# w_in loaded in f32 chunks and cast on chip, V of batch 0 summed per head pair, cast engines chosen anew

## The chip, the core and the metric

The kernel runs on one core of a Trainium2 chip. A core has TensorE (PE, matrix products, with weight loads shown apart as PEld), VectorE (DVE), ScalarE (ACT), GpSimd (POOL) and SyncE (SP), which here only issues DMAs. TensorE writes to PSUM; the other data lives in SBUF, 128 partitions wide. The metric is the device time of one execution in microseconds, lower is better. The kernel before took 215.6 us in the median of six runs (213.97 to 217.12).

## The reference

Attention with a causal window of 64 keys (8 batches, 8 heads, 576 positions, head size 64), followed by a gated unit that mixes positions with a spatial matrix. All inputs and the output are float32.

```python
def _attn_ref(q, k, v):
    scores = np.matmul(q, k.transpose(0, 1, 3, 2)) / np.sqrt(64)
    rel = pos[:, None] - pos[None, :]
    scores = np.where((rel >= 0) & (rel < 64), scores, -1e9)
    attn = np.exp(scores - np.max(scores, axis=-1, keepdims=True))
    attn = attn / (np.sum(attn, axis=-1, keepdims=True) + 1e-09)
    return np.matmul(attn, v)

def _moe_ref(x, w_in, w_spatial, b_spatial, w_out):   # x: (8, 576, 512)
    h = np.maximum(x @ w_in, 0.0)                     # w_in: 512 x 1024
    u, v = h[..., :512], h[..., 512:]
    v_n = (v - mean(v)) / np.sqrt(var(v) + 1e-06)     # over the last axis
    v_s = np.einsum('ts,bsd->btd', w_spatial, v_n) + b_spatial[None, :, None]
    return (u * v_s) @ w_out                          # w_out: 512 x 512
```

## The kernel before, in words

Nothing is scheduled automatically. One string, `ORDER` (line 20), lists some 1,150 steps; lines 644 to 646 read it word by word and call the function that each word names, with the numbers after the dots as arguments. Each engine runs its own instructions in exactly that order, so the string fixes all queues at once: a step that waits holds back everything behind it on its engine. A last letter P, D or A puts a copy on POOL, DVE or ACT.

The work of a batch `b`:

- **Loads** on SP: `l.b.x.s` (load, line 288; x is q or k) and `lv.b.n` (line 304). Batches 0 to 2 come in pieces of a head pair (s = 0 to 3, 256 KB, rows of 1 KB) and one piece with the last 64 positions of all heads (s = 4, 128 KB). From batch 3 on q and k come in eight pieces of one head (144 KB). V comes in pieces n, of one head (128 KB) or of 128 positions (256 KB). The f32 buffers (tags fq, fk, vf) exist twice, so batch b+2 waits for the casts of batch b.
- **Casts** to f16: `c.b.x.s.e` (line 317) for q and k, 512 elements wide per partition in batches 0 to 2 and 1152 wide after that; `cv.b.n.e` (line 330) for V; `sh.b.n.half.e` (line 339) copies V shifted by 64 rows.
- **Attention** of a head pair s (s = 4 is the last 64 positions of all): in batches 0 to 2 `T.b.x.s` transposes on TensorE and `to.b.x.s.e` copies the result out of PSUM; later `R.b.x.s` transposes on DVE. Then `S.b.s` scores on TensorE, `E.b.s` exp on ACT (tile e), `M.b.s` the mask as a minimum on DVE, `P.b.s` sums and values on TensorE (tile oz), `n1` and `n2` ln and exp on ACT (tiles ln, zi), `x.b.s` the product on DVE (tile x), which is pair s of the input to the gated unit.
- **Gated unit**: `V.b.j.r0.r1` (line 517) is 128 positions j times the right half of w_in; the sum over the 512 input columns runs in four parts r, part r being head pair r, and r0 to r1 says which of the parts are done by this word. `Q.b` does the last 64 positions of V and the last 64 of the output of the batch before. `vo` evicts V with a relu (tile vs), `bs` takes its mean and variance on DVE, `rs` and `ln` normalise it (tile vn). `U.b.m` (line 575) is the left half of w_in times x (tile pu), `ru` its relu on ACT. `G.b.m` is the spatial product (tile ps), `g` the gate on DVE, `O.b.j` the output product (tile po), `oc.b.j.e` (line 620) its copy into an f32 buffer (tag ob, five buffers), `st.b.j` (line 627) the store on SP.
- **Weights**: `win.half` (k_win, line 243) loads half of w_in with one gpsimd DMA that casts to f16 on the way. `wsp` and `wout` do so with the other two; `W.kk` and `wo.kk.e` turn the spatial matrix.
- **Warm-ups**: `H.n` runs n matmuls on a scratch tile.

Batch b's gated unit is interleaved with the attention of batch b+1 and the loads of later ones. In the order before, every `c`, `cv` and `sh` is on POOL but for five casts of batch 0, every `oc` on ACT, and every `vo` on ACT but for four. Eight SP DMAs can be in flight, each with a semaphore of its own: a ninth load waits for the landing of the one eight places before it.

The two halves of w_in were placed behind P of pair 0; V of batch 0 comes in the pieces 0 to 3 and 3 to 4:

```
... c.0.k.2.D lv.0.6 ... c.0.q.3.D win.1 H.3 to.0.q.1.A lv.0.8 n2.0.0 c.0.k.3.D win.0 ...
V.0.2.0.3 ... V.0.0.0.3 ... V.0.3.0.3 ... V.0.2.3.4 ... V.0.3.3.4 ... V.0.0.3.4 ... V.0.1.0.3 ... V.0.1.3.4
```

Of the kernel before, what the change touches and what calls it, by code (L numbers as in the profile page):

```python
# [14 lines left out]
S = 576  # L15
# [5 lines left out]
keep scratch l.0.k.1 H.4 id l.0.q.2 l.0.k.0 l.0.q.0 lv.0.0 H.6 l.0.k.2 lv.0.3 c.0.k.1.D lv.0.1 mask  # L21
c.0.q.2.P lv.0.2 H.3 maskr l.0.q.3 c.0.k.0.D c.0.q.0.P ones.0 l.0.q.4 T.0.k.0 l.0.k.3 to.0.k.0.D
T.0.q.0 l.0.q.1 H.2 to.0.q.0.A c.0.k.2.D lv.0.6 T.0.k.1 H.3 l.1.k.1 to.0.k.1.D S.0.0 l.1.q.0
cv.0.0.P E.0.0 sh.0.0.0.P lv.0.7 sh.0.0.1.P M.0.0 lv.0.5 cv.0.1.P small lv.0.4 P.0.0 sh.0.1.1.P
n1.0.0 T.0.k.2 c.0.q.1.P table T.0.q.2 lv.1.0 to.0.k.2.D sh.0.1.0.P T.0.q.1 l.0.k.4 c.0.q.3.D win.1
H.3 to.0.q.1.A lv.0.8 n2.0.0 c.0.k.3.D win.0 lv.1.2 to.0.q.2.A S.0.1 x.0.0 c.0.q.4.P l.1.q.1 H.2
E.0.1 T.0.q.3 cv.0.3.P lv.1.1 T.0.k.3 S.0.2 to.0.q.3.A l.1.k.0 M.0.1 cv.0.2.P E.0.2 to.0.k.3.D P.0.1
sh.0.2.0.P n1.0.1 H.2 M.0.2 sh.0.3.0.P S.0.3 n2.0.1 H.4 E.0.3 x.0.1 lv.1.3 c.0.k.4.P sh.0.2.1.P
P.0.2 M.0.3 n1.0.2 sh.0.3.1.P T.0.q.4 n2.0.2 T.0.k.4 P.0.3 to.0.q.4.A x.0.2 cv.0.4.P n1.0.3
V.0.2.0.3 to.0.k.4.D c.1.q.0.P n2.0.3 V.0.0.0.3 sh.0.4.0.P ones.1 x.0.3 l.1.k.3 S.0.4 c.1.k.1.P  # L30
V.0.3.0.3 E.0.4 wsp V.0.2.3.4 lv.1.4 M.0.4 V.0.3.3.4 vo.0.2.A V.0.0.3.4 T.1.q.0 vo.0.3.D l.1.k.2
vo.0.0.A P.0.4 l.1.q.2 bs.0.3 n1.0.4 U.0.1 to.1.q.0.A c.1.q.1.P bs.0.2 n2.0.4 V.0.1.0.3 ru.0.1
l.1.k.4 x.0.4 V.0.1.3.4 T.1.q.1 l.1.q.3 vo.0.1.D c.1.k.0.P Q.0 to.1.q.1.A T.1.k.1 cv.1.0.P vo.0.4.A
T.1.k.0 to.1.k.1.D U.0.0 cv.1.1.P to.1.k.0.D sh.1.0.1.P bs.0.4 S.1.0 U.0.4 sh.1.1.0.P E.1.0 bs.0.0
S.1.1 sh.1.0.0.P U.0.3 E.1.1 bs.0.1 sh.1.1.1.P lv.1.5 U.0.2 ru.0.0 M.1.1 ru.0.3 l.1.q.4 M.1.0 rs.0
W.0 ru.0.4 ln.0.4 P.1.1 wo.0.A ln.0.3 P.1.0 lv.1.6 ru.0.2 W.4 c.1.k.2.P n1.1.1 lv.1.7 wo.4.D W.1
c.1.q.2.P ln.0.0 W.2 l.2.q.0 wo.1.A wout T.1.k.2 wo.2.A lv.1.8 W.3 ln.0.1 ln.0.2 n1.1.0 l.2.k.0
c.1.k.3.P wo.3.D G.0.1 l.2.k.2 to.1.k.2.D n2.1.0 cv.1.2.P l.2.k.1 n2.1.1 T.1.q.2 g.0.1 T.1.k.3
c.1.q.3.P lv.2.2 G.0.0 to.1.q.2.A x.1.1 to.1.k.3.D G.0.2 cv.1.3.P g.0.0 c.1.q.4.P T.1.q.3 x.1.0
sh.1.2.1.P G.0.3 to.1.q.3.A g.0.2 c.2.q.0.P c.1.k.4.P S.1.2 g.0.3 S.1.3 lv.2.3 E.1.2 sh.1.2.0.P  # L40
T.1.q.4 T.1.k.4 G.0.4 to.1.k.4.D sh.1.3.0.P lv.2.1 to.1.q.4.A M.1.2 O.0.0 E.1.3 cv.1.4.P T.2.q.0
oc.0.0.A M.1.3 S.1.4 l.2.q.4 P.1.2 E.1.4 c.2.k.0.P g.0.4 lv.2.8 O.0.2 to.2.q.0.A M.1.4 sh.1.3.1.P
n1.1.2 l.2.q.3 T.2.k.0 O.0.1 n2.1.2 l.2.k.4 to.2.k.0.D sh.1.4.0.P l.2.q.1 oc.0.2.A x.1.2 P.1.3
l.2.q.2 c.2.k.1.P P.1.4 n1.1.3 lv.2.0 cv.2.1.P S.2.0 n1.1.4 O.0.3 l.2.k.3 oc.0.1.A n2.1.3 c.2.q.4.P
lv.2.4 V.1.1.0.2 n2.1.4 cv.2.4.P V.1.0.0.2 x.1.3 oc.0.3.A lv.2.5 V.1.1.2.3 c.2.k.2.P x.1.4 V.1.0.2.3
E.2.0 V.1.1.3.4 V.1.0.3.4 st.0.2 vo.1.1.D V.1.2.0.2 c.2.k.4.P vo.1.0.A V.1.2.2.3 l.3.k.5 M.2.0
T.2.k.1 V.1.3.0.2 c.2.q.1.P to.2.k.1.D V.1.3.2.3 V.1.3.3.4 V.1.2.3.4 c.2.q.3.P vo.1.3.D U.1.0 lv.3.1
vo.1.2.A sh.2.1.1.P bs.1.1 l.3.k.3 T.2.q.1 ru.1.0 c.2.q.2.P T.2.q.3 l.3.q.1 U.1.1 bs.1.2 to.2.q.1.A
cv.2.0.P to.2.q.3.A T.2.k.2 sh.2.0.1.P T.2.q.2 ru.1.1 to.2.k.2.D S.2.1 sh.2.1.0.P to.2.q.2.A Q.1
bs.1.3 E.2.1 lv.2.6 sh.2.0.0.P l.3.k.1 bs.1.0 P.2.0 c.2.k.3.P vo.1.4.A l.3.q.2 T.2.q.4 cv.2.2.P  # L50
n1.2.0 S.2.2 st.0.3 bs.1.4 T.2.k.3 oc.0.4.A sh.2.2.1.P U.1.3 lv.2.7 n2.2.0 M.2.1 st.0.0 U.1.2
to.2.q.4.A l.3.k.2 to.2.k.3.D rs.1 E.2.2 l.3.k.0 x.2.0 U.1.4 l.3.q.0 T.2.k.4 ln.1.2 ru.1.3 P.2.1
ln.1.0 ln.1.1 ru.1.4 l.3.q.4 S.2.3 ru.1.2 ln.1.3 ln.1.4 G.1.0 n1.2.1 l.3.q.3 to.2.k.4.D n2.2.1 G.1.4
E.2.3 x.2.1 cv.2.3.P G.1.2 lv.3.3 M.2.2 sh.2.3.1.P g.1.0 S.2.4 G.1.1 E.2.4 M.2.3 sh.2.2.0.P g.1.4
G.1.3 lv.3.0 M.2.4 sh.2.3.0.P g.1.2 P.2.2 lv.3.2 g.1.1 sh.2.4.0.P P.2.3 n1.2.2 g.1.3 O.1.2 c.3.q.0.P
n2.2.2 l.4.k.0 n1.2.3 x.2.2 P.2.4 l.3.q.6 cv.3.1.P n2.2.3 O.1.1 l.3.k.7 c.3.k.0.P oc.1.2.A x.2.3
st.0.1 V.2.3.0.4 n1.2.4 l.3.k.4 R.3.q.0 n2.2.4 cv.3.0.P l.3.q.5 V.2.1.0.4 x.2.4 sh.3.0.1.P st.0.4
R.3.k.0 V.2.0.0.4 l.3.q.7 vo.2.1.A l.3.k.6 cv.3.2.P vo.2.3.A S.3.1 oc.1.1.A cv.3.3.P bs.2.3 l.4.q.0
S.3.0 E.3.1 sh.3.1.1.P V.2.2.0.4 bs.2.1 l.4.k.3 E.3.0 U.2.0 l.4.k.5 sh.3.1.0.P vo.2.0.A M.3.0
l.4.q.3 O.1.3 vo.2.2.A sh.3.0.0.P bs.2.0 O.1.0 M.3.1 Q.2 c.3.q.1.P oc.1.0.A bs.2.2 ru.2.0 st.1.0  # L60
P.3.0 vo.2.4.A l.4.k.1 P.3.1 c.3.k.1.P R.3.q.1 oc.1.3.A l.4.q.1 U.2.1 n1.3.0 st.1.1 bs.2.4 n2.3.0
l.4.k.2 U.2.3 R.3.k.1 st.1.2 oc.1.4.A l.4.q.2 ru.2.1 U.2.4 x.3.0 rs.2 U.2.2 lv.3.4 ru.2.3 ln.2.1
ln.2.0 n1.3.1 S.3.2 ln.2.2 ru.2.2 ln.2.3 lv.4.3 ln.2.4 G.2.0 ru.2.4 n2.3.1 G.2.1 E.3.2 x.3.1 g.2.0
c.4.k.0.P lv.4.2 S.3.4 S.3.3 g.2.1 E.3.4 G.2.4 M.3.2 E.3.3 lv.4.0 c.4.q.0.P G.2.3 g.2.4 M.3.3 G.2.2
lv.4.1 cv.3.4.P P.3.2 cv.4.3.P g.2.2 l.4.k.7 P.3.3 sh.3.4.0.P l.4.k.6 g.2.3 n1.3.3 O.2.2 l.4.k.4
R.4.q.0 cv.4.2.P n1.3.2 l.4.q.7 O.2.0 R.4.k.0 sh.4.1.1.P n2.3.2 st.1.3 n2.3.3 l.4.q.4 O.2.1 x.3.2
l.4.q.6 x.3.3 cv.4.1.P V.3.3.0.4 l.4.q.5 oc.2.1.A cv.4.0.P M.3.4 oc.2.2.A lv.5.2 S.4.0 sh.4.0.1.P
vo.3.3.A S.4.1 oc.2.0.A bs.3.3 P.3.4 V.3.1.0.4 n1.3.4 l.5.q.1 c.4.k.1.P V.3.2.0.4 l.5.k.2 vo.3.1.A
sh.4.1.0.P R.4.k.1 n2.3.4 l.5.q.2 O.2.3 E.4.0 x.3.4 st.1.4 bs.3.1 sh.4.0.0.P V.3.0.0.4 vo.3.2.A
l.5.q.5 M.4.0 E.4.1 l.5.k.3 U.3.3 c.4.q.1.P bs.3.2 l.5.k.4 oc.2.3.A Q.3 vo.3.0.A l.5.k.0 cv.5.2.P  # L70
R.4.q.1 P.4.0 vo.3.4.A l.5.k.7 bs.3.0 S.4.2 n1.4.0 l.5.k.6 bs.3.4 U.3.1 n2.4.0 E.4.2 l.5.k.1 x.4.0
U.3.0 l.5.q.3 M.4.1 rs.3 S.4.3 l.5.k.5 ru.3.3 ln.3.1 P.4.1 ln.3.2 ru.3.1 l.5.q.0 ln.3.3 oc.2.4.A
U.3.2 ln.3.0 ln.3.4 E.4.3 lv.4.4 M.4.2 G.3.0 n1.4.1 M.4.3 ru.3.2 G.3.2 n2.4.1 ru.3.0 x.4.1 P.4.2
lv.5.3 c.5.k.0.P g.3.2 n1.4.2 G.3.1 l.5.q.6 g.3.0 n2.4.2 st.2.1 U.3.4 x.4.2 st.2.2 c.5.k.1.P G.3.3
st.2.0 ru.3.4 g.3.1 l.5.q.7 R.5.k.0 c.5.q.0.P S.4.4 l.5.q.4 P.4.3 g.3.3 lv.5.0 n1.4.3 G.3.4 cv.4.4.P
n2.4.3 O.3.3 sh.4.4.0.P E.4.4 x.4.3 V.4.2.0.4 cv.5.3.P R.5.q.0 oc.3.3.A sh.5.1.0.P O.3.0 g.3.4
vo.4.2.A M.4.4 lv.5.1 O.3.1 sh.5.1.1.P oc.3.0.A P.4.4 l.6.q.5 S.5.0 n1.4.4 st.3.3 n2.4.4 S.5.1
c.5.q.1.P E.5.0 st.2.3 x.4.4 V.4.0.0.4 R.5.k.1 lv.6.1 oc.3.1.A cv.5.0.P l.6.k.1 V.4.1.0.4 R.5.q.1
vo.4.0.A st.2.4 M.5.0 O.3.2 lv.5.4 vo.4.1.A cv.5.1.P E.5.1 bs.4.1 V.4.3.0.4 sh.5.0.1.P bs.4.0 S.5.2
l.6.q.0 vo.4.3.A sh.5.0.0.P l.6.q.2 Q.4 bs.4.2 oc.3.2.A l.6.q.3 bs.4.3 l.6.k.3 P.5.0 vo.4.4.A U.4.1  # L80
# [31 lines left out]
def kernel(  # L112
# [51 lines left out]
    G = {}  # L164
# [512 lines left out]
```

## Time and profile before

| | us |
|---|---|
| median of six runs | 215.6 |
| the profiled execution, total | 216.5 |
| its span, first to last instruction | 214.8 |
| TensorE busy | 199.9 |
| DVE busy | 154.6 |
| ACT busy | 155.0 |
| POOL busy | 110.4 |
| warm-up matmuls on TensorE (29) | 11.3 |
| first V matmul of batch 0 starts | 24.7 |
| first U matmul of batch 0 starts | 29.3 |
| last matmul of the kernel ends | 210.6 |

The profile is one execution; its total of 216.5 us stands 0.9 us above the median of the runs. Its slices cut the span into 40 parts of 5.4 us, and a digit is the busy share of a part in tenths. PEclk is the clock that TensorE was granted. The chain of waits follows the work that ended last back to the start, at each step to what released it. A busy matmul is modelled to its end, and matmuls overlap, so busy time overstates what TensorE did.

The rows of the operations that the change moves (mean of one, by shape):

| operation | engine | ns |
|---|---|---|
| q or k cast, 512 f32 to f16 | POOL | 639 to 650 |
| the same | DVE | 418 to 425 |
| q or k cast, 1152 wide | POOL | 1145 to 1307 |
| V cast, 512 wide | POOL | 609 to 636 |
| shift copy, 64 x 512 f16 | POOL | 637 to 705 |
| shift copy, 64 x 1024 f16 | POOL | 1055 to 1101 |
| relu eviction vs, 512 wide | ACT / DVE | 604 / 684 |
| output eviction ob, 512 wide | ACT | 584 |

### The profile page before, as it was taken

The page shows a single profiled execution, that of the slowest core. Times are in us where ns is not written, and L with a number is a line of the kernel's source. Part 1 is how long each engine was busy: PE and PEld are TensorE (multiplying, and loading weights), DVE is VectorE, ACT ScalarE, POOL GpSimd, SP SyncE. Part 2 cuts the span into 40 slices and gives each one's busy share as a digit, 9 for nine tenths or more (in the row PEclk, how much of TensorE's full clock was granted, in tenths as well). Part 3 has the DMA queues.
Part 4 walks back from the last instruction along what each step waited for, and adds up shares of the span by engine and source line. Part 5 has one row for each costly group of instructions (what it writes and reads, how often), then busy time and mean ns, then how long its engine had stood idle before and what let it go on. Part 6 is the DMA issues. An engine that isn't in the chain of part 4 may idle for free.

```text
span 214.8 us, 6725 instructions
## 1 busy us (share of the span) xinstructions
PE 199.9 (93%) x2766; PEld 106.7 (50%) x2766; DVE 154.6 (72%) x298; ACT 155.0 (72%) x289; POOL 110.4 (51%) x152
## 2 busy tenths in 40 slices
PE   7749899999999999999889899899999999999992
PEld 2325455655465454555354455365555555454540
DVE  3444588985998969785999659886787899747530
ACT  3478886948798578847797588775994799586532
POOL 3289598577945884275709840796006962000000
PEclk9985999999999999999999999999999999999999
DMA  5999999999999992999999999970899944000524
GB/s 153 267 259 191 248 256 219 227 231 190 263 222 221 218 234 69 257 209 246 218 205 266 160 253 191 275 196 3 181 249 227 170 136 140 34 5 2 185 86 169
DMA packets 79215, 40.43 MB, mean 188 GB/s; under 512 B 43280, under 2 KB 74576, under 8 KB 79184
## 3 DMA queue, kind: packets, MB, share of 16 engines
q1 hardware_dynamic: 76960, 37.76, 81.0%
q0 software_dynamic: 2224, 2.24, 6.4%
q8 instruction: 21, 0.34, 0.8%
q14 instruction: 10, 0.08, 0.2%
HBM read 32.79 MB, written 9.44 MB: 197 GB/s over the span
## 4 chain that ended last, share of the span: by engine, by line
PE 56%; ACT 13%; DMA 13%; SPq 6%; DVE 6%; issue 2%; POOL 1%; POOLq 0%
PE ps L603 14%; PE po L617 11%; PE pv L522 10%; DMA vf<-in_v_dram 6%; PE pu L580 5%; DMA fk<-in_k_dram 5%; ACT zi L500 3%; PE sc L412 3%; PE oz L477 3%; DMA fq<-in_q_dram 3%; ACT ob L624 2%; PE pv L534 2%; ACT e L444 2%; SPq L301 2%; ACT ru L593 2%; ACT ln L493 2%
## 5 line engine op out<-in xcount | busy, mean ns | idle before, releaser
L603 PE MATMUL ps<-wspT,vn 128*128 128x512 f16 (+1 forms) x256 | 39.0, 286 | 0.9 <-DVE vn L571 0.7
L508 DVE TENSOR_TENSOR x<-oz,zi 128x512 f16<-128x512 f32 (+1 forms) x40 | 25.0, 628 | 16.7 <-ACT zi L500 16.5
L444 ACT ACTIVATE e<-sc 128x1024 f16<-128x1024 f32 x32 | 32.5, 1027 | 4.3 <-PE sc L401 4.1
L493 ACT ACTIVATE ln<-oz 128x512 f32<-128x512 f32 (+1 forms) x40 | 22.1, 558 | 17.9 <-PE oz L487 17.7
L617 PE MATMUL po<-wout,g 128*128 128x512 f16 x128 | 31.6, 380 | 1.0 <-ACT e2r L449 0.8
L337 POOL CAST vn<-vf 128x512 f16<-128x512 f32 (+1 forms) x28 | 17.4, 628 | 28.8 <-DMA vf<-in_v_dram 16.0
L553 DVE BATCH_NORM_STATS2 st<-vs 128x6 f32<-128x512 f16 (+1 forms) x40 | 26.9, 673 | 7.1 <-ACT vs L547 7.0
L522 PE MATMUL pv<-win,x 128*128 128x512 f16 x128 | 31.2, 380 | 0.6 <-DVE x L508 0.6
L460 DVE TENSOR_TENSOR e<-e,mask 128x1024 f16<-128x1024 f16 x32 | 26.6, 834 | 6.8 <-ACT e L444 6.6
L580 PE MATMUL pu<-x,win 128*128 128x512 f16 x128 | 31.2, 380 | 0.0
L610 DVE TENSOR_TENSOR g<-ps,ru 128x512 f16<-128x512 f32 (+1 forms) x40 | 24.3, 629 | 6.4 <-PE ps L603 6.1
L547 ACT ACTIVATE vs<-pv 128x512 f16<-128x512 f32 (+1 forms) x36 | 21.1, 601 | 10.1 <-PE pv L522 8.2
L624 ACT COPY ob<-po 128x512 f32<-128x512 f32 (+1 forms) x33 | 19.2, 584 | 10.1 <-PE po L617 9.6
L500 ACT ACTIVATE zi<-ln 128x512 f32<-128x512 f32 (+1 forms) x40 | 23.3, 591 | 0.9
L603 PEld LDWEIGHTS <-vn 128*128 128x128 f16 x256 | 16.6, 97 | 14.4 <-DVE vn L571 2.4
L593 ACT ACTIVATE ru<-pu 128x512 f32<-128x512 f32 (+1 forms) x40 | 21.1, 555 | 1.5 <-PE pu L580 1.0
L328 POOL CAST nk<-fk 128x1152 f16<-128x1152 f32 x10 | 13.0, 1307 | 14.4 <-DMA out_dram<-ob 6.8
L351 POOL COPY vs<-vn 64x512 f16<-64x512 f16 (+1 forms) x22 | 19.4, 885 | 1.3
L522 PEld LDWEIGHTS <-x 128*128 128x128 f16 x128 | 11.7, 98 | 14.7 <-DVE x L508 1.8
L617 PEld LDWEIGHTS <-g 128*128 128x128 f16 x128 | 11.6, 97 | 13.8 <-DVE g L610 1.0
L349 POOL COPY vs<-vn 64x512 f16<-64x512 f16 (+1 forms) x22 | 17.8, 827 | 0.5
L580 PEld LDWEIGHTS <-win 128*128 128x128 f16 x128 | 11.5, 97 | 12.5 <-issue 0.6
(103 smaller groups left out, 340.6 us busy)
## 6 DMA issues: line engine op xcount, KB each, us to landing
out_dram<-ob SPq DMA_DIRECT2D x32, 256.0 KB, 3.1
fk<-in_k_dram SPq DMA_DIRECT2D x40, 144.0 KB, 5.0
fq<-in_q_dram SPq DMA_DIRECT2D x40, 144.0 KB, 5.0
vf<-in_v_dram SPq DMA_DIRECT2D x20, 256.0 KB, 6.1
vf<-in_v_dram SPq DMA_DIRECT2D x32, 128.0 KB, 5.7
fk<-in_k_dram SPq DMA_DIRECT2D x12, 256.0 KB, 5.7
fq<-in_q_dram SPq DMA_DIRECT2D x12, 256.0 KB, 5.7
win<-in_moe_w_in_dram POOLq DMA_DIRECT2D x2, 512.0 KB, 8.4
```

The source lines that it names most:

```text
L444: nc.scalar.activation(e2[:, :, :], sc[0][:, :, :], AF.Exp, bias=0.0, scale=0.125)
L460: nc.vector.tensor_tensor(e2[:, :, :], e2[:, :, :], m, ALU.min)
L493: nc.scalar.activation(lnz[:, 0:n], OZ[b, s][:, 1, 0:n], AF.Ln)
L500: nc.scalar.activation(zinv[:, 0:n], lnz[:, 0:n], AF.Exp, bias=0.0, scale=-1.0)
L508: nc.vector.tensor_tensor(x[:, 0:n], oz[:, 0, 0:n], zinv[:, 0:n], ALU.mult)
L522: nc.tensor.matmul(PV[b, j][0:jn, :], xcol(b, r, j), w_in_sb[:, r, 512:1024], start=(r == 0), stop=(r == 3))
L553: nc.vector.bn_stats(st6[0:jn, 0:6], VSB[b, j][0:jn, :])
L580: nc.tensor.matmul(pu[:, :], w_in_sb[:, r, 128 * m:128 * m + 128], X[b, r][:, :], start=(r == 0), stop=(r == 3))
L593: nc.scalar.activation(RU[b, m][:, 0:n], pu[:, 0:n], AF.Relu)
L603: nc.tensor.matmul(o, VN[b, kk][0:kn, 128 * mm_:128 * mm_ + 128], w, start=(kk == 0), stop=(kk == 4))
L610: nc.vector.tensor_tensor(g[:, :], ps[:, 0:n], RU.pop((b, m))[:, 0:n], ALU.mult)
L617: nc.tensor.matmul(po[:, :], G[b, r][:, 128 * j:128 * j + 128], w_out_sb[:, r, :], start=(r == 0), stop=(r == 3))
```

## The change

The one `win` word per half goes. Two new steps take its place: `wl.half.r` loads 128 rows of half of w_in, 256 KB in f32 with rows of 2 KB, on the sync queue into a buffer of the tag ob (shared with the output copies, five in all), and `wc.half.r.e` casts it to f16 on the engine e.

```diff
-    WP = {}
+    WP, WF = {}, {}
...
-    def k_win(half):
+    def wl(half, r):
         cs = slice(512 * half, 512 * half + 512)
-        nc.gpsimd.dma_start(w_in_sb[:, :, cs], moe_w_in[:, cs].rearrange("(r p) c -> p r c", p=128))
+        WF[half, r] = new(mpool, [128, 512], f32, "ob", 5, f"wf{half}_{r}")
+        nc.sync.dma_start(WF[half, r][:, :], moe_w_in[128 * r:128 * r + 128, cs])
+
+    def wc(half, r, e):
+        COPY[e](w_in_sb[:, r, 512 * half:512 * half + 512], WF.pop((half, r))[:, :])
```

The whole of `ORDER` is replaced by another. It holds the same steps with other places and other engines. Its SP queue begins as follows (before above, after below), with the loads of batch 0 and the chunks:

```diff
-l.0.k.1 l.0.q.2 l.0.k.0 l.0.q.0 lv.0.0 l.0.k.2 lv.0.3 lv.0.1 lv.0.2 l.0.q.3 l.0.q.4 l.0.k.3 l.0.q.1
-lv.0.6 l.1.k.1 l.1.q.0 lv.0.7 lv.0.5 lv.0.4 lv.1.0 l.0.k.4 lv.0.8 lv.1.2 l.1.q.1 lv.1.1 l.1.k.0
...
+l.0.k.0 l.0.k.1 l.0.q.0 l.0.k.3 l.0.q.1 lv.0.0 l.0.q.3 l.0.k.2 lv.0.3 lv.0.1 wl.1.1 l.0.q.2 lv.0.2
+lv.0.4 wl.1.3 l.0.q.4 lv.0.5 l.0.k.4 lv.0.6 lv.0.7 wl.1.0 lv.0.8 l.1.k.1 wl.1.2 wl.0.0 l.1.q.1
+wl.0.1 wl.0.3 lv.1.0 lv.1.1 l.1.q.0 l.1.k.0 wl.0.2 l.1.k.3 lv.1.2 lv.1.3 l.1.q.3 l.1.k.2
...
```

TensorE's queue, from the scores of pair 0 to the end of batch 0's U:

```diff
-S.0.0 P.0.0 T.0.k.2 T.0.q.2 T.0.q.1 H.3 S.0.1 H.2 T.0.q.3 T.0.k.3 S.0.2 P.0.1 H.2 S.0.3 H.4 P.0.2
-T.0.q.4 T.0.k.4 P.0.3 V.0.2.0.3 V.0.0.0.3 S.0.4 V.0.3.0.3 V.0.2.3.4 V.0.3.3.4 V.0.0.3.4 T.1.q.0
-P.0.4 U.0.1 V.0.1.0.3 V.0.1.3.4 T.1.q.1 Q.0 T.1.k.1 T.1.k.0 U.0.0 S.1.0 U.0.4 S.1.1 U.0.3 U.0.2
...
+S.0.0 S.0.1 T.0.k.2 T.0.k.3 T.0.q.3 P.0.0 T.0.q.2 H.3 S.0.2 P.0.1 T.0.q.4 H.4 T.0.k.4 S.0.3 P.0.2
+V.0.1.0.1 V.0.1.1.2 V.0.0.0.1 V.0.3.0.1 V.0.3.1.2 P.0.3 V.0.0.1.2 V.0.3.2.3 V.0.0.2.3 S.0.4
+V.0.2.0.1 V.0.2.1.2 V.0.1.2.3 V.0.0.3.4 V.0.3.3.4 V.0.2.2.3 V.0.2.3.4 V.0.1.3.4 T.1.k.1 T.1.q.1
+T.1.q.0 P.0.4 T.1.k.0 S.1.1 U.0.1 U.0.0 S.1.0 Q.0 U.0.4 U.0.3 U.0.2
...
```

The chunks are cast as `wc.1.3.D`, `wc.1.1.D` (in that order, behind `x.0.0`), `wc.1.0.P`, `wc.1.2.P`, `wc.0.0.P`, `wc.0.2.A`, `wc.0.1.P` and `wc.0.3.A`. Of the copies whose engine is a letter in the order:

| step | before P / D / A | after P / D / A |
|---|---|---|
| c | 45 / 5 / 0 | 33 / 5 / 12 |
| cv | 40 / 0 / 0 | 17 / 9 / 14 |
| sh | 52 / 0 / 0 | 30 / 7 / 15 |
| to | 0 / 15 / 15 | 0 / 14 / 16 |
| vo | 0 / 4 / 36 | 0 / 16 / 24 |
| oc | 0 / 0 / 40 | 0 / 13 / 27 |
| wo | 0 / 2 / 3 | 0 / 3 / 2 |
| wc | none | 4 / 2 / 2 |

The ACT table is now loaded by the first instruction of ACT; before, the profile shows three table loads. The warm-up matmuls are 29 in both.

## The prediction

> **What bounds the kernel now.** First the page's busy times, slices and chain.
>
> ```profile
> PE 199.9 (93%) x2766; PEld 106.7 (50%) x2766; DVE 154.6 (72%) x298; ACT 155.0 (72%) x289; POOL 110.4 (51%) x152
> ...
> PE   7749899999999999999889899899999999999992
> ...
> PEclk9985999999999999999999999999999999999999
> ...
> DMA  5999999999999992999999999970899944000524
> ...
> PE 56%; ACT 13%; DMA 13%; SPq 6%; DVE 6%; issue 2%; POOL 1%; POOLq 0%
> ```
>
> TensorE is busy for 93% of the span. It is short of work in the third and fourth slices (11 to 22 us), where its clock also drops, and at the end. POOL, which now does nearly all casts, is idle half the time and holds 1% of the chain. Next the windows view, one row for each stretch:
>
> ```profile
> 0.00:24.60 24.60, 18.70 (x205) 9.52 (x205) 10.77 (x27) 14.99 (x22) 14.09 (x28) 0.86 1.04 215
> 24.60:40.00 15.40, 14.41 (x192) 8.06 (x187) 12.47 (x26) 12.52 (x25) 12.49 (x21) 1.00 1.20 243
> 40.00:100.00 60.00, 59.65 (x901) 32.81 (x901) 49.14 (x91) 45.93 (x88) 39.05 (x54) 1.00 1.06 216
> 100.00:140.00 40.00, 36.85 (x550) 19.20 (x540) 32.41 (x59) 31.02 (x58) 22.82 (x25) 1.00 1.08 223
> 140.00:210.00 70.00, 69.70 (x944) 37.00 (x941) 49.85 (x97) 49.71 (x99) 21.92 (x26) 1.00 0.53 126
> ```
>
> After the length come PE, PEld, DVE, ACT, POOL, the clock, the DMA share and GB/s. TensorE lacks 6.9 us before 40 us, 3.2 us from 100 to 140 us, 0.7 us elsewhere up to 210 us. Before 24.6 us most of its work is warm-ups. So two stages can give something back: the start, and 100 to 140 us, where the chain of waits reads:
>
> ```profile
> 105.14 4.84 DMA fk<-in_k_dram
> 109.98 0.02 issue
> 109.99 6.42 DMA vf<-in_v_dram
> 116.42 0.02 issue
> 116.43 6.52 DMA vf<-in_v_dram
> 122.96 0.05 issue
> 123.01 0.63 POOL vn L337
> ```
>
> There loads set the pace; POOL's cast that frees a buffer for the next load is a short link. "Busy" flatters TensorE: a 512-column matmul averages 379 ns in its group, yet four take 0.86 us in the chain (216 ns each). The mid stages hide some slack, so a longer vector chain can still show.
>
> **What the Trainium skill says.** "DMA: Bandwidth & Descriptors", section "Issuing engines are not separate DMA queues": DMAs of all engines share the same 16 DMA engines, and another issuer saves only issue time. The trace agrees: the gpsimd queue's 2.24 MB is 6.4% of the engines' span, beside 81.0% for sync. "SBUF — State Buffer", section "Who interferes with whom": VectorE in a two-port mode and GpSimd exclude each other for whole instructions. The trace fits: a mask minimum on DVE is 692 ns in the median and 2310 ns at most. Fewer POOL casts mean fewer such collisions, more DVE copies mean more. "TensorE: Matmul & The Clock Gate", Part 1: an idle TensorE falls to half clock. The trace shows 0.70 in 10 to 20 us.
>
> **The change part by part.**
>
> *w_in on sync.* Removed: two gpsimd DMAs, 1.64 us of POOL at 15.71 us, and their share of the DMA engines, 6.4% x 214.8 us x 1.05/2.24 MB = 6.4 us. Added: eight 256 KB loads. At the sync queue's mean (37.76 MB in 81.0% of 214.8 us, 217 GB/s) the 2.1 MB cost 9.7 us; at the 2 KB-row stores' rate in the tail (slices of 370 to 390 GB/s) 5.5 us. Net -0.9 to +3.3 us of DMA time. I take +0.5: a chunk's rows are 2 KB too. The issues cost 8 x 0.47 = 3.8 us of SP, which from 11 us waits on landings anyway (single issues of 1 to 4 us); loads queued behind are priced with the landings. The sixth chunk reuses the first's buffer and waits for its DVE cast, put after x.0.0: about 18.5 us below, while that load's turn comes about 19 us. If it misses, batch 1's loads slip by the same amount.
>
> *V of batch 0.* Before: first pv at 24.7 us, first pu at 29.3, last pu of batch 0 ends at 37.3. Batch 0 landed at about 4.5 us per MB from 2.1 us on (2.75 MB by 14.6 us). In the new order q of pair 1 is the fifth load (1.31 MB, 8 us; it was the thirteenth, cast at 14.59), so S.0.1 needn't wait till 17.08. K, Q, V of the pairs and r=1, r=3 of the V half put pair 2's P at about 21 us (23.1 before) and x.0.3 at 25.3 (27.2 before). The eight r=0 and r=1 matmuls (8 x 216 ns = 1.7 us) run in that wait. V would end near 27 us; before, taking out the U group and small work between (1.3 us), near 29.9. That is 2.9 us earlier. What is late next: T.1.q.0 and U. The query load of batch 1's pair 0 is the thirty-first (6.42 MB, seven chunks in front), the last U chunk the thirty-third (6.95 MB). With chunks at 2.75 us per MB they land at 27.8 and 29.7 us; at 4.5, at 31.0 and 33.4. After cast, U.0.1 can start near 30 or 33 us; U, S and Q behind it need 5.2 to 5.7 us: end 35.6 to 39.2 against 37.3. So **-1.7 to +1.9 us; I take -1.5**, near the fast end for the row size.
>
> *Casts, shifts and evictions moved.* Counts from the two orders, durations from the rows of before. A 512-wide f32 to f16 ACT copy isn't shown: I take ob's 0.58 us, wider ones plus 0.83 ns per element (e: 1024 in 1.03 against 0.60 for 512). ACT gains 6 narrow and 6 wide q/k casts (3.5 + 6.7), 14 V casts (8.1), 8 narrow and 7 wide shifts (4.6 + 7.1), 2 chunks and one tr copy (1.8), loses 13 ob, 12 vs, one wspT (7.6 + 7.2 + 0.7): +16.3, to 171. DVE gains 9 V casts (9 x 0.425), 7 shifts (about 0.3 each by the 512-wide mask copy of 0.29), a wide cast (0.8), 2 chunks (0.85), 13 ob and 12 vs (25 x 0.684), one wspT, loses a narrow cast and a tr copy: +24, to 179. POOL loses about 43 us, to 67. Added load lies beside TensorE unless it closes a chain. Lower bound: only windows at 9 of 10 or above overflow. From 60 to 70 us DVE was 9.10 and gains 24 x 10/214.8 = 1.1; from 150 to 160 ACT was 9.43 and gains 0.8: 0.4 us together. Upper bound: growth spread over the chain, 13% x 214.8 x 16.3/155 = 2.9 on ACT and 6% x 214.8 x 24/154.6 = 2.0 on DVE, 4.9 us. I take **+0.5**: most ACT and DVE time has slack in the windows.
>
> *100 to 140 us.* A cast on DVE takes 0.43 us against POOL's 0.63, and two or three engines free buffers side by side. The order of loads and stores is new throughout, which the old trace can't price: at best the 3.2 us go; at worst a store queued earlier holds loads back, as the SP idles of 4.3 us before 83 us and 8.6 us before 150 us did; I allow +2. I take **-1.5**.
>
> *At nothing.* Two fewer ACT table loads (1.28 us each at 11.2 and 13.5 us): ACT then idled 1.14 us for tp_1q. The 29 warm-ups stay 29, placed anew. The tail past 210 us keeps its last matmul, copy and store.
>
> Sum: -1.5 + 0.5 - 1.5 = -2.5 us. The profiled execution took 216.5 us (span 214.8); less 2.5 is 214.0. The median of the runs is 215.6, 0.9 lower, so 213.1; I say **213.0**.
>
> **Rivals.**
> *A, ACT and DVE become the bound*: place, the chain E, mask, P, ln, exp, x of each pair, above all 60 to 75 us and 150 to 160 us; price, the full 4.9 us, with the start giving nothing: 215.6 + 4.9 = 220.5, or with the start's -1.5, 219. It decides once those stretches pass 9.5 on both engines and TensorE has gaps behind x. For it: 80% and 83% mean load. Against: POOL gave the chain only 1%, but each shortened cast also comes off a wait.
> *B, the start is taken back*: chunks land at the sync mean, TensorE waits at T.1.q.0 or U till 33 us and its clock drops: +1.9 at the start, -1.5 and +0.5 later, 216.5, within 1%.
> *C, the search pays in the hidden slack*: the new order also fills waits that "busy" covers. If the 100 to 140 us loss goes whole and 2 us more, with the start at -1.5: 215.6 - 6.7 + 0.5, about 209.5. For it: 216 ns pace against 379. Against: nothing in the old trace shows the new order.
>
> **How the numbers follow.** Forecast 0.33 (211 to 215), A 0.30, B 0.18, C 0.19. The range 208.0 to 220.5 reaches from a little below C to A's full price. I count 1% (213.4 and 217.8) as about what a measurement can tell. Faster takes C and most of the forecast, 0.44; the same takes B and the rest, 0.26; slower takes A, 0.30. The forecast's own range is 211 to 215.
>
> **What would show it.** First pv near 22 us and last pu of batch 0 before 36 us: the start is right; a TensorE idle of 2 us or more before 33 us at tp of batch 1 or at pu: B. ACT near 171, DVE near 179, POOL near 67 busy us: the counts are right. TensorE's idle from 100 to 140 us under 2 us: the third step holds; idle behind x or e in the mid stages: A. DMA near 41.5 MB with the same saturated stretches confirms the transfer's price. I am wrong if TensorE starts V early and the gain is gone by 60 us.

## The result, and the profile after

The changed kernel takes 217.1 us in the median of 28 runs, the kernel before 215.2 us in 63. The ratio is **1.0094 [1.0071, 1.0116]**; measured a second time (run e15) it was 1.0044 [1.0015, 1.0073] (217.2 against 215.6 us). So it is slower by half to one per cent, where 213.0 us and a gain of 1.2% were forecast: the sign was wrong. (Ratios leave out the runs that are more than 1.5% above the fastest of their kernel, medians do not, so the two can differ by up to 0.7%.)

The profiled execution took 218.3 us, 1.2 us above its median; that of before stood 1.3 us above its own. The lines of the page that answer to those shown of before:

```profile
span 216.6 us, 6758 instructions
PE 199.0 (92%) x2766; PEld 105.6 (49%) x2766; DVE 172.6 (80%) x341; ACT 168.5 (78%) x305; POOL 70.6 (33%) x97
...
PE   7765989899999996999999999999899999999992
...
PEclk9999699999999999999999999999999999999999
DMA  5999999899999999999699999979629963011314
...
PE 49%; DVE 12%; ACT 11%; SPq 10%; DMA 10%; issue 3%; POOL 2%; ACTq 0%; POOLq 0%
```

The counts came out nearly as worked out: ACT 168.5 (171 expected), DVE 172.6 (179), POOL 70.6 (67). The new hole in the row of PE is its sixteenth digit, a 6, near 84 us. In the chain TensorE fell from 56% to 49%, and DVE rose from 6% to 12%. The windows view (after the length PE, PEld, DVE, ACT, POOL, clock, DMA share, GB/s):

```profile
0.00:24.60 24.60, 17.89 (x202) 9.15 (x204) 13.69 (x34) 14.99 (x22) 10.61 (x24) 0.94 1.00 244
24.60:40.00 15.40, 14.44 (x202) 8.01 (x197) 11.35 (x25) 13.47 (x29) 9.97 (x17) 0.98 1.01 237
40.00:100.00 60.00, 56.25 (x823) 30.87 (x824) 55.01 (x102) 51.84 (x96) 24.87 (x34) 1.00 1.10 222
100.00:140.00 40.00, 39.78 (x596) 20.97 (x596) 36.22 (x73) 36.52 (x63) 10.73 (x12) 1.00 1.05 211
140.00:210.00 70.00, 68.24 (x950) 35.79 (x947) 56.31 (x111) 49.62 (x95) 14.43 (x15) 1.00 0.52 127
```

From 100 to 140 us TensorE now lacks 0.2 us instead of 3.2. That gain is real, but 3.8 us are missing between 40 and 100 us (0.4 before) and 1.8 us after 140 us (0.3 before). Two single waits, 1.88 and 1.42 us, make up most of this. The first, in the timeline (start, us, engine, instruction; in brackets the idle time before it):

```profile
80.61 1.38 POOL L355 COPY vs<-vn 64x1024 f16<-64x1024 f16 x1
81.83 3.44 DVE L466 TENSOR_TENSOR e<-e,mask 128x1024 f16<-128x1024 f16 x1
81.94 1.14 POOL L334 CAST nk<-fk 128x1152 f16<-128x1152 f32 x1
83.03 1.14 POOL L334 CAST nq<-fq 128x1152 f16<-128x1152 f32 x1
84.12 0.60 POOL L343 CAST vn<-vf 128x512 f16<-128x512 f32 x1
85.33 0.41 PE L483 MATMUL oz<-e,onesK 128*64 128x512 f16 x2 [1.88 <-DVE e L466]
```

The mask `M.3.1` takes 0.69 us when it is alone. Here it runs until 0.55 us after the end of the fourth POOL copy in a row, and `P.3.1` on TensorE waits 1.88 us for it. The second wait, in the same view:

```profile
149.24 1.03 ACT L355 COPY vs<-vn 64x1024 f16<-64x1024 f16 x1
149.31 1.04 PE L586 MATMUL pu<-x,win 128*128 128x512 f16 x4
...
150.17 1.92 ACT L450 ACTIVATE e<-sc 128x1024 f16<-128x1024 f32 x2
...
151.99 0.58 ACT L599 ACTIVATE ru<-pu 128x512 f32<-128x512 f32 x1
...
152.62 1.24 PE L623 MATMUL po<-wout,g 128*128 128x512 f16 x5 [1.42 <-ACT ru L599]
```

The shift copy `sh.6.0.0`, which the change moved from POOL to ACT, stands ahead of two exps, and these ahead of the relu `ru.5.0`, after whose end `O.4.1` starts.

**Lost time.** Idle time hides behind busy matmuls, as the prediction said, so I use a second measure worked out from the traces. For each word of the order on TensorE, warm-ups aside, take the time from its first matmul to the next word's first; subtract what words of its kind need (the fifteenth percentile of such words over six traces: before, after and the first four experiments); warm-ups count in full. The sum is the time lost, by stage in us. How finely kinds are told apart moves all rows together, so only the differences between rows count:

| kernel | to 40 | 40 to 100 | 100 to 140 | after 140 | all |
|---|---|---|---|---|---|
| before | 18.8 | 3.1 | 5.3 | 2.6 | 29.9 |
| changed | 18.4 | 6.5 | 1.8 | 4.9 | 31.7 |
| changed, second trace (e15) | 17.4 | 4.6 | 2.3 | 4.8 | 29.1 |
| e3: new order, old engines | 17.9 | 6.3 | 2.0 | 2.6 | 28.8 |
| e5: one shift back on POOL | 17.3 | 5.3 | 1.9 | 4.0 | 28.4 |
| e6: late copies back | 17.2 | 6.3 | 2.2 | 3.0 | 28.8 |
| e12: that shift later on ACT | 16.7 | 3.8 | 1.9 | 4.4 | 26.8 |
| e13: early copies back | 17.8 | 5.7 | 2.1 | 4.9 | 30.5 |
| e11: copies back from 73 us on | 16.6 | 4.6 | 2.1 | 2.4 | 25.7 |

Its totals follow the spans (before to changed: +1.8 us both ways). Rows two, three, five, six and seven have the same instructions up to about 140 us, and still differ by up to 1.7 us before 40 us and 2.7 us from there to 100 us: that is chance of the single execution. From 100 to 140 us, and after 140 us for like letters, traces agree to 0.6 us.

### The profile page after: what moved, and what is told of

It is laid out like the page before. It is cut to its first block, busy times and chain, and to the rows that moved or that the text cites. A ratio compares the mean times of both kernels' runs of the same rounds, so it can differ in the third digit from the quotient of the medians.

```text
span 216.6 us, 6758 instructions
## 1 busy us (share of the span) xinstructions
PE 199.0 (92%) x2766; PEld 105.6 (49%) x2766; DVE 172.6 (80%) x341; ACT 168.5 (78%) x305; POOL 70.6 (33%) x97
## 4 chain that ended last, share of the span: by engine, by line
PE 49%; DVE 12%; ACT 11%; SPq 10%; DMA 10%; issue 3%; POOL 2%; ACTq 0%; POOLq 0%
PE ps L609 14%; PE po L623 10%; PE pv L528 7%; PE pu L586 6%; PE sc L418 3%; DMA wf<-in_moe_w_in_dram 3%; DVE st L559 3%; SPq L314 3%; DMA fk<-in_k_dram 3%; PE oz L483 3%; ACT e L450 2%; SPq L298 2%; DVE e L466 2%; PE pv L540 2%; PE oz L493 2%
## 5 line engine op out<-in xcount | busy, mean ns | idle before, releaser
L528 PE MATMUL pv<-win,x 128*128 128x512 f16 x128 | 32.9, 390 | 0.3 <-DVE x L514 0.3
L466 DVE TENSOR_TENSOR e<-e,mask 128x1024 f16<-128x1024 f16 x32 | 27.9, 876 | 4.6 <-ACT e L450 4.5
L553 ACT ACTIVATE vs<-pv 128x512 f16<-128x512 f32 (+1 forms) x24 | 13.8, 592 | 5.0 <-PE pv L528 3.3
L334 POOL CAST nq<-fq 128x1152 f16<-128x1152 f32 x7 | 8.3, 1187 | 28.1 <-DMA fq<-in_q_dram 25.7
L609 PE MATMUL ps<-wspT,vlast 65*128 65x512 f16 (+1 forms) x64 | 17.3, 288 | 0.0
L343 POOL CAST vn<-vf 128x512 f16<-128x512 f32 (+1 forms) x11 | 7.7, 700 | 29.1 <-DMA vf<-in_v_dram 29.1
L355 POOL COPY vs<-vn 64x512 f16<-64x512 f16 (+1 forms) x14 | 12.5, 891 | 11.7 <-PE pv L528 4.3
L483 PE MATMUL oz<-e,onesK 128*64 128x512 f16 x64 | 13.1, 403 | 3.0 <-DVE e L466 1.9
```

Of the source, the lines that this page charges most:

```text
L466: nc.vector.tensor_tensor(e2[:, :, :], e2[:, :, :], m, ALU.min)
L528: nc.tensor.matmul(PV[b, j][0:jn, :], xcol(b, r, j), w_in_sb[:, r, 512:1024], start=(r == 0), stop=(r == 3))
L609: nc.tensor.matmul(o, VN[b, kk][0:kn, 128 * mm_:128 * mm_ + 128], w, start=(kk == 0), stop=(kk == 4))
```

## The experiments

Theory 1: the moved copies cost because ACT and DVE carry more as a whole. Theory 2: their load is harmless, and single copies at single places make another engine late. Theory 3 is, in e1 to e4, that the w_in chunks cost; from e7 on, that loads set the pace up to 140 us, so that what is won at one wait is lost at the next load.

**e1 to e4: which part of the change costs.** The two orders and the two sets of engine letters are crossed, and w_in goes back to gpsimd.

```diff
e1  before's order:  -c.6.k.0.P  +c.6.k.0.A   (all letters as changed, win on gpsimd)
e2  before's order:  -win.1 win.0  +wl.1.1 wc.1.1.D ...   (letters as before)
e3  changed order:   -sh.6.0.0.A  +sh.6.0.0.P   (all common letters as before, chunks kept)
e4  changed order:   -wl.* wc.*  +sh.0.1.1.P win.1 win.0   (letters as changed)
```

> The order of before, word for word, with only the engine letters of c, cv, sh, to, vo, oc and wo taken from the changed kernel; w_in stays two gpsimd DMAs. Theory 1 (the moved copies overload ACT and DVE): 1% to 2% slower than before, DVE near 172 and ACT near 168 busy us, TensorE idle behind mask, x or relu in the mid stages. Theory 2 (the load is harmless, the new order's stalls at single places cost): within 0.7% of before. Theory 3 (w_in by chunks costs): within 0.5%, since w_in is not touched.

> The order and engines of before, with w_in in eight f32 chunks at the same ranks among the loads as in the changed kernel and cast on the same engines. Theory 3: 0.7% or more slower, first pu of batch 0 later than 29.3 us by 2 us or more. Theories 1 and 2: within 0.5% of before, the delay at the start is absorbed by 53 us.

> The changed kernel with the engine letters of before put back for every copy that both have; order and chunks as changed. Theory 1: 1% or more faster than the changed kernel (215 us or less against 217.1), DVE back near 155. Theory 2: not faster; the order was made for spread casts, so POOL, again with all casts, comes late: 217 to 222 us. Theory 3: as the changed kernel, 217.

> The changed kernel with w_in loaded again by two gpsimd DMAs that cast, issued behind the shift copies of pair 1; no chunk loads, no chunk casts; order and engines else as changed. Theory 3: 0.7% or more faster than the changed kernel. Theories 1 and 2: first pv moves from 21.7 to about 25 us, batch 0's U ends within 1 us of 36.8, and the time stays within 0.5% of the changed kernel.

| run | median us | ratio to before |
|---|---|---|
| e1 | 228.0 | 1.0588 [1.0527, 1.0649] |
| e2 | 221.3 | 1.0287 [1.0232, 1.0342] |
| e3 | 216.5 | 1.0017 [0.9985, 1.0049] |
| e4 | 220.2 | 1.0262 [1.0204, 1.032] |

The before's median beside them was 215.3 us. In an order that was not made for them, both parts cost much: the letters 5.9%, more than any theory had expected, and the chunks 2.9%. In the new order gpsimd w_in, at the place that e4 gives it, is the worse choice, so the chunks don't carry the loss there. The letters do: with the old ones (e3) the new order is level with the kernel before.

**e5: one letter.** The changed kernel with the shift of the second wait back on POOL.

```diff
-sh.6.0.0.A
+sh.6.0.0.P
```

> The changed kernel with one letter changed: the wide shift of batch 6, pair 0 (sh.6.0.0) goes from ACT back to POOL. Theory 2 (the load is harmless, single places cost): TensorE's 1.79 us wait before O.4.1 at 152.6 us goes, nothing after it waits for loads, so the end comes 1.3 to 1.9 us earlier: about 215.4 us, ratio 1.001 to the kernel before. Theory 1 (ACT and DVE are overloaded as a whole): 1.0 us of 168.5 us of ACT cannot be seen; 217.1 us, ratio 1.009.

Measured: 0.9996 [0.9969, 1.0023], medians 215.9 against 215.4 us. The wait before `O.4.1` fell from 1.42 to 0.48 us:

```profile
149.37 0.81 PE L627 MATMUL po<-wout,g 128*128 128x512 f16 x3 [0.48 <-ACT ru L603]
```

The trace explains 0.94 us of gain; the ratio says 2.1 us against the first measurement of the changed kernel and 1.0 us against the second.

**e6 and e13: late letters, early letters.** e6 puts the 22 common copies behind `S.5.4` (142 us) back on their old engines; e13 does so with all those ahead of it.

```diff
e6   ... S.5.4 ...  -sh.6.1.1.A cv.6.1.D vo.5.2.D ...  +sh.6.1.1.P cv.6.1.P vo.5.2.A ...
e13  -c.1.q.3.A cv.3.3.A oc.1.2.D ...  +c.1.q.3.P cv.3.3.P oc.1.2.A ...  S.5.4 ...
```

> The changed kernel with the engines of the kernel before for the 22 common copies that stand after S.5.4 (about 142 us) in the order; everything ahead as in the changed kernel. Theory 2: the waits before O.4.1 (1.79 us) and G.5.1 (0.57 us) go, the rest stays: 2.3 us, about 214.8 us, ratio 0.998, and TensorE's other waits after 140 us stay where they are. Theory 1: the cost of the moved copies is spread in proportion, 22 of some 80 letters, at most 0.5 us: 216.6 us, ratio 1.007.

> The changed kernel with the engines of the kernel before for all common copies ahead of S.5.4 (about 142 us), behind it as changed: the complement of the kernel with the late engines back. If the late letters carry the cost (Theory 2), this one keeps the waits before O.4.1 and G.5.1 and is 1% or more slower than the kernel with old engines throughout: 217 to 218.5 us, ratio 1.008 to 1.015. If the load of the early copies carries it (Theory 1), it is close to that kernel: 216.5 us, ratio 1.002.

e6 measured 0.9919 [0.9888, 0.9951] (medians 215.2 against 215.4 us), e13 1.0106 [1.0046, 1.0167] (218.9 against 215.6). The windows from 140 to 205 us, first e6:

```profile
140.00:205.00 65.00, 64.52 (x904) 33.98 (x901) 46.44 (x94) 47.14 (x95) 21.58 (x26) 1.00 0.52 125
```

and e13:

```profile
140.00:205.00 65.00, 63.22 (x875) 32.68 (x872) 53.19 (x105) 48.10 (x92) 13.56 (x14) 1.00 0.52 127
```

TensorE lacks 0.5 us in e6 and 1.8 us in e13; in the changed kernel it lacks 1.8 us. In e13 `O.4.1` waits again, in the view of waits (what waited, for what, us, times, longest):

```profile
PE po L627 <- ACT ru L603: 1.4, 1, 1.4
PE ps L613 <- ACT ru L603: 0.2, 1, 0.2
```

The lost time after 140 us is 4.8 to 5.1 us with the new late letters (changed, e15, e13, and e7 and e8 below), 2.4 to 3.0 us where they are old (e3, e6, e11). So the late letters cost about 2.2 us in the traces; the ratios say 0.9% (e13 against e3) and 1.3 to 1.8% (the changed kernel against e6), 1.9 to 3.8 us. The early ones don't cost: e6 against e3, and the changed kernel against e13, are if anything faster with them. Theory 1 falls with this, since 89 of the 111 changed letters, most of the moved load, are early ones.

**e12 and e14: is it the shift itself?** e12 leaves it on ACT but behind `ru.5.0`. e14 puts it, as the only new letter behind 73 us, into the kernel of e11 (below).

```diff
e12  -sh.6.0.0.A vo.5.2.D ... ru.5.0
     +vo.5.2.D ... ru.5.0 sh.6.0.0.A
e14  -sh.6.0.0.P
     +sh.6.0.0.A
```

> The changed kernel with the wide shift sh.6.0.0 left on ACT, but four ACT instructions later in the order, behind the relu ru.5.0 and no longer ahead of the exps E.6.0 and E.6.1. ACT's load and every engine letter are as changed. Theory 2 (the place in the queue costs): the wait before O.4.1 falls from 1.42 us to 0.5 us or less, as it did with the shift on POOL, and the end comes 1 to 2 us earlier than the changed kernel: about 215.5 us, ratio 1.000 to 1.005. Theory 1 (ACT's load costs): no change, 217.1 us, ratio 1.009. If it is no faster though the wait is gone, P.6.0 (behind the shift) has become the next wait.

> The kernel with old engines from 73 us on (ratio 0.994), with one letter changed: the wide shift of batch 6, pair 0 on ACT, as in the changed kernel. Theory 2, the wait of the trace alone: O.4.0 or O.4.1 waits for ru.5.0 about 1 us longer than there, 0.4 to 0.5% slower, ratio 0.998 to 0.999. If the single letter is worth what putting it back brought in the first run (1.0%): ratio 1.004. Theory 1: 0.994.

e12 measured 1.0062 [1.0031, 1.0093] (217.0 against 214.6 us), not clearly better than the changed kernel. The wait went down, and another one came up behind the moved copy:

```profile
PE po L627 <- ACT ru L603: 0.5, 1, 0.5
PE po L627 <- ACT ob L634: 0.4, 1, 0.4
```

The eviction `oc.4.2` now stands behind the shift. e14 measured 0.9936 [0.9902, 0.997] against 0.9939 for e11: in company of old letters the same shift at the same place of ACT's queue costs nothing. That is Theory 1's figure; the wait that Theory 2 expected is not there. In its trace the shift (from 150.21 us), an eviction and the two exps hold `ru.5.0` up even longer, until 154.02 us, and TensorE does all twelve matmuls of `O.4.2`, `O.4.1` and `O.4.0` meanwhile:

```profile
151.16 2.75 PE L627 MATMUL po<-wout,g 128*128 128x512 f16 x12
...
153.44 0.58 ACT L603 ACTIVATE ru<-pu 128x512 f32<-128x512 f32 x1
...
154.08 0.63 PE L595 MATMUL pu<-x,win 128*128 128x64 f16 x16 [0.16 <-ACT ru L603]
```

What differs is which step waits for the relu. `O.4.1` does not use its result. But the products of V, U, G and O share four PSUM buffers (the tag mm), and the programs built from these kernels list, in every one with the new late letters (changed, e4, e5, e7, e8, e10, e12, e13, e15), `O.4.1` in the buffer that the relu has to read out first. With old late letters (e3, e6, e11) it is `O.4.0` that gets this buffer, and in e14 `U.5.4`. So the letters (between e11 and e14 a single one) also decide which product gets which buffer. From the first matmul of `O.4.2` to the first of `O.4.1` TensorE takes 2.43 to 2.44 us in the seven traces with the late letters and the shift as changed (changed, e4, e7, e8, e10, e13, e15), 1.51 us in e5 and e12, and 0.86 us in e3, e6, e11 and e14. The cost needs both, a relu held up in ACT's queue and a product that needs its buffer soon. Which other late letter moves the buffer was not tried.

**e7: the mask without POOL beside it.**

```diff
-M.3.1 U.2.0 c.3.k.1.P ... c.3.q.1.P
+M.3.1 U.2.0 c.3.k.1.D ... c.3.q.1.D
```

> The changed kernel with the two wide casts of batch 3, pair 1 (c.3.k.1, c.3.q.1) on DVE behind the mask M.3.1 and no longer on POOL beside it. Theory 2: M.3.1 takes under 1.5 us instead of 3.44, TensorE's wait of 2.08 us before P.3.1 goes, and the end comes up to 2 us earlier: about 215.2 us, ratio 1.000. Theory 3 (up to 140 us the loads set the pace, so time won at one wait is lost at the next one for a load): the wait before P.3.1 goes, but TensorE waits again between 90 and 140 us, and the end stays: 216.5 to 217.1 us, ratio 1.006 to 1.009. Theory 1: no change, 217.1 us.

Measured 1.0083 [1.0047, 1.0119]. `M.3.1` now took 0.70 us and `P.3.1` did not wait:

```profile
83.77 0.70 DVE L470 TENSOR_TENSOR e<-e,mask 128x1024 f16<-128x1024 f16 x1
84.40 1.16 DVE L338 CAST nk<-fk 128x1152 f16<-128x1152 f32 x1
```

That part of Theory 2 holds. But nothing was won: with the two casts DVE came late with the x that `S.3.2` waits for, before which the time from one matmul's start to the next grew from 0.71 to 1.82 us. The end is as Theory 3 said, for a reason that is not its own: the queue that took the work, not a load.

**e15: the changed kernel again.**

> The changed kernel itself, on the same chip as the two others. Both theories: 217 us, ratio 1.007 to 1.012. In its trace, if the mask wait before P.3.1 is an accident of timing (a mask that starts a little earlier or later meets fewer POOL copies), it is not 2.08 us again but anywhere from 0.2 to 2 us, and TensorE's loss between 40 and 100 us moves with it; if it belongs to the order it is 2 us again.

Measured 1.0044 [1.0015, 1.0073]. With the same instructions the mask was held for 1.80 us, not 3.44:

```profile
80.68 1.80 DVE L470 TENSOR_TENSOR e<-e,mask 128x1024 f16<-128x1024 f16 x1
80.79 1.14 POOL L338 CAST nk<-fk 128x1152 f16<-128x1152 f32 x1
82.19 1.30 POOL L338 CAST nq<-fq 128x1152 f16<-128x1152 f32 x1 [0.25 <-DMA fq<-in_q_dram]
...
82.53 0.41 PE L487 MATMUL oz<-e,onesK 128*64 128x512 f16 x2 [0.23 <-DVE e L470]
```

The load of q landed a little later, POOL paused for 0.25 us, and the mask got in. TensorE's wait is 0.23 us instead of 1.88. So the size of the first wait is an accident of timing; the second was 1.41 to 1.42 us in both traces of the changed kernel and in e13.

**e9 and e10: less DMA.** The same shortening of the stores in both kernels, which leaves out seven of eight output rows of batches 0 to 3.

```diff
-jn = 128 if j < 4 else 64
+jn = (128 if j < 4 else 64) // (8 if b < 4 else 1)
```

> The kernel before with the stores of batches 0 to 3 cut to the first 16 of their 128 rows (8 of 64 in the last tile): the rest of those rows of the output is left out, 4.1 of 40.4 MB of DMA; every issue and wait stays. Theory 3 (up to 140 us the loads set the pace): the wait that TensorE has from 100 to 140 us, 3.2 us idle, shrinks by most of it, and the end comes 2 to 4 us earlier: about 212.4 us, ratio 0.987. Theory 2 (single waits between engines): at most 0.5 us, 215 us, ratio 0.998.

> The changed kernel with the same stores cut in the same way. Theory 3: TensorE's waits from 40 to 100 us are the same load wait moved forward; they shrink, and the end comes 2 to 4 us earlier than the changed kernel: about 214 us, ratio 0.995. Theory 2: the waits before 100 us (mask, x, copies) hang on DVE, ACT and POOL and stay, the waits after 140 us stay too: 216.6 to 217.1 us, ratio 1.007 to 1.009.

e9 measured 0.9995 [0.9955, 1.0035], e10 1.0226 [1.0164, 1.0287]. Theory 3 falls. In the kernel before, the loads left the chain; its line in e9:

```profile
PE 63%; ACT 15%; DVE 12%; SPq 3%; DMA 2%; issue 2%; POOL 0%; DVEq 0%; POOLq 0%
```

DMA was 13% before. But TensorE still lost 5.0 us from 100 to 140 us, because the casts came at other times and met DVE's normalisation:

```profile
110.33 3.09 DVE L571 TENSOR_SCALAR vn<-vs,mv,rs 128x512 f16<-128x512 f16 x4
110.77 2.51 POOL L328 CAST nk<-fk 128x1152 f16<-128x1152 f32 x2 [6.58 <-DMA fk<-in_k_dram]
113.22 1.20 POOL L328 CAST nq<-fq 128x1152 f16<-128x1152 f32 x1
...
113.48 1.04 PE L603 MATMUL ps<-wspT,vn 128*128 128x512 f16 x4 [1.26 <-DVE vn L571]
```

In e10 DVE was late for TensorE in the same way between 40 and 100 us (8.5 us lost against 6.5 and 4.6 in the two traces of the changed kernel), in the view of waits:

```profile
PE oz L483 <- DVE e L466: 1.8, 2, 1.3
PE ps L609 <- DVE vn L577: 1.3, 3, 0.8
```

**e8: V of batch 0 in one go per tile.**

```diff
-V.0.1.0.1 V.0.1.1.2 ... V.0.1.2.3
+... V.0.1.0.3
```

> The changed kernel with V of batch 0 summed over the first three head pairs in one go for each output tile, where the piece of the third pair stood, in place of pair by pair; everything else as changed. If the split is worth what the start gained (V's matmuls of pairs 0 and 1 lie in the wait for pair 2's x): 8 x 0.22 = 1.7 us fall behind x.0.2, V of batch 0 ends 1.0 to 1.7 us later than 28.3 us and so does U, and the run ends at 218 to 218.8 us, ratio 1.013 to 1.017. If the start is bound by the landings behind it or by other waits (Theory 3): V ends later but U does not, 217.1 us, ratio 1.009. Faster than that if the small pieces themselves cost (each piece shows a gap of 0.2 us at its first matmul): below 217 us.

Measured 1.0159 [1.0102, 1.0217], medians 218.5 against 215.4 us. The interval lies just at the end of that of the first measurement and above that of the second, so the split is likely worth a half to one per cent, as its 1.7 us of matmuls suggested. Where it is won is not shown, since the trace does not show it at the start: batch 0's U ended at 36.3 us, between the two traces of the changed kernel (36.8 and 35.7).

**e11: the best of both.** New order and start, old letters for the 51 common copies behind `P.2.2` (73 us).

```diff
... P.2.2  -sh.2.4.0.A cv.3.3.A oc.1.2.D ...  +sh.2.4.0.P cv.3.3.P oc.1.2.A ...
```

> The changed kernel with the engines of the kernel before for the 51 common copies that stand after P.2.2 (about 73 us) in the order, ahead of it as changed. It joins the new order, the start and the first 73 us as changed, and what followed in the kernel with old engines throughout, without that one's wait of 2.4 us before and in G.1.0. Theory 2: TensorE's waits before O.4.1 and G.5.1 go, and the mask M.3.1 meets no POOL burst as long as the old engines keep it apart: 2.3 us to 4 us better than the changed kernel, 213 to 214.8 us, ratio 0.989 to 0.998. Theory 1 (load): between the kernel with old engines throughout and the changed one: 216.6 us, ratio 1.004.

Measured **0.9939 [0.9905, 0.9973]**, medians 214.5 against 215.9 us: faster than both kernels by ratio and median; e6 is level with it by the ratio alone. Its windows:

```profile
40.00:100.00 60.00, 58.67 (x865) 32.05 (x870) 52.74 (x98) 49.74 (x93) 31.36 (x41) 1.00 1.12 227
100.00:140.00 40.00, 39.43 (x652) 21.20 (x641) 32.35 (x63) 32.48 (x64) 24.62 (x28) 1.00 1.08 232
140.00:205.00 65.00, 64.86 (x863) 33.93 (x861) 44.48 (x92) 46.13 (x91) 18.61 (x21) 1.00 0.50 121
```

After 140 us TensorE lacks 0.1 us. In these stages DVE and ACT carry 15 and 9 us less than in the changed kernel's windows up to 205 us (144.6 and 137.1 us), POOL 25 us more, and no TensorE wait over 0.1 us is listed after 140 us.

## Why the prediction was wrong

**The failing step: the term for casts, shifts and evictions moved, taken at +0.5 us.** It measured about 2.2 us, all after 140 us (lost time 4.8 to 5.1 against 2.4 to 3.0 us), and putting those 22 letters back turned the sign (e6, 0.9919). The counts of instructions and the busy sums were right; the pricing was not. The step added copies to windows and charged only what overflowed a stretch at nine tenths. Of the 2.2 us, 1.6 us lie at one place that no such sum sees (2.44 against 0.86 us between `O.4.2` and `O.4.1`): a copy of 1.03 us stood on ACT ahead of two exps and a relu, and with these letters the next product had to wait for the PSUM buffer that this relu reads. ACT was busy there without a pause for some 4 us, but for only 49.6 of the 70 us of that stage; and in e14 the relu came later still and TensorE lost 0.16 us. The prediction had no term for who waits for what. Its upper bound, 4.9 us, did hold the cost, by luck, for it was worked out from a growth of the whole chain.

**The stage without a term, 40 to 100 us.** The prediction priced the start and 100 to 140 us and left what lies between out of the sum. In the five traces with the same order and letters there the lost time is 3.8 to 6.5 us, mean 5.3, against 3.1 us: +2.2, as far as one trace of before can tell. It seems to come with the new order, since e3 with old letters loses 6.3. The prediction named the collisions of DVE with POOL and put no price on them. The masks' busy sum did shrink, from 33.5 to 32.7 us, but where a collision falls decides, and that changes from run to run. Why the new order loses more here is not settled.

**V of batch 0, taken -1.5: about right.** First pv at 21.7 us, in e15 at 20.8 (about 22 expected); V ended at 28.4 us, in e15 at 26.1 (near 27 expected). Lost time up to 40 us, over the changed kernel's two traces, e5, e6, e7 and e12, which start alike: 18.4, 17.4, 17.3, 17.2, 18.5, 16.7, mean 17.6, against 18.8: -1.2. The profiled execution was one of the poor ones, with U's end at 36.8 us (35.7 in e15, under 36 expected) and a clock digit of 6 in the slice from 21.7 us.

**100 to 140 us, taken -1.5: the gain came, the reason did not.** Lost time went from 5.3 to 1.8 to 2.3 us, the idle time from 3.2 to 0.2 us, with old letters too (e3: 2.0). So the order of steps brought it, not faster casts, and the right sign of this term was partly luck. "Loads set the pace" was read off the chain of waits; e9 took the loads out of that chain and won nothing.

**w_in on sync, taken +0.5: can't be told apart, and isn't the cause.** Queues q1 and q0 held the DMA engines for 87.4% of 214.8 us before, 187.7 us, and 85.7% of 216.6 us after, 185.6 us, while the whole moved 1.04 MB more. In the new order gpsimd w_in is slower by about 2% (e4). The prediction's sum of three terms does not hold this +0.5, and does not say that the start's term covers it; with it the sum is -2.0 us.

**The sum again.** -1.2 (start) + 2.2 (40 to 100 us) - 3.3 (100 to 140 us) + 2.2 (late letters) = -0.1 us against a profiled execution of before that stood 1.3 us above its median. The prediction took that offset off both sides. Without it the changed kernel stands 1.2 us over before's median, where the ratios make it 1.0 (second measurement) to 2.0 us (first).

**The rivals.** A had the place (150 to 160 us) and the sign, but not the mechanism: ACT and DVE were not the bound there: from 150 to 155 us, where TensorE waited, they were busy for 3.0 and 4.4 of 5 us. B is refuted: TensorE waited little before 33 us at batch 1's transposes or at U (single steps lose 0.4 to 0.9 us), and the start's gain stayed; that its 216.5 us is the nearest figure is luck. C was not seen in the changed kernel; e11 gets part of it.

## What to carry to other kernels

Before you move a copy to another in-order engine, write down what stands behind it in that queue and who waits for that, for a result or for a buffer: the load of the engine does not tell. Then look again in the new program, since the move can also change which product gets which buffer. Letters and order belong together: the same letters cost 5.9% in another order, and in their own the late ones cost 0.9 to 1.8% and the early ones nothing, so put a search's choices back one half at a time before you keep them. And a DMA in the chain of waits is the last releaser of one execution, not a bound: take bytes away before you believe it.

## What the runs showed of the hardware

- A mask minimum (two f16 inputs in SBUF) on DVE was never longer than 0.69 us where no POOL instruction overlapped it in time (306 in 17 traces). Beside one it took up to 3.44 us, over 1 us in 113 of 374. The normalisation of vn (0.40 us) went up to 1.78 us. The products x and g, with one input in PSUM, and the variance sums, with one input, never passed 0.70 us with POOL beside them (680 and 311). That agrees with the Trainium skill, "SBUF — State Buffer", section "Who interferes with whom", which lets two SBUF inputs and the two-port modes contend with GpSimd and nothing else; the mask falls under the first, not under the two-port modes that the prediction named. Beyond the page, the mask did not get in between four POOL instructions in a row; only a pause of POOL let it in (0.25 us in e15).
- Taking DMA away can cost time: 4.1 of 41.5 MB less made the changed kernel slower, 1.0226 against 1.0044 and 1.0094. In e10's trace TensorE waits 1.8 us for masks and 1.3 us for vn between 40 and 100 us, in e15's 0.2 and 0.2 us; that this is the whole reason is not shown.
- Two executions of the changed kernel lost 6.5 and 4.6 us between 40 and 100 us. A single trace shows which waits exist; how much they cost needs a second one.
